# Up and down products of the later chunks: seven-product block sums in float32 exchanged for three float32r products

## The chip, the cores and the metric

The kernel runs on one core of a Trainium2 chip. The metric is the device time of one launch in microseconds, the median of several runs; smaller is better. The kernel before takes 517.86 us (two runs, 517.85 and 517.86). Its profiled execution has a span of 515.2 us from the first to the last instruction, and a mean granted TensorE clock of 0.992.

## The reference, cut to what matters

A gated linear-attention cell (mLSTM) for 4 batches and 8 heads of 40 channels over 768 steps is followed by a feed-forward layer with an exact GELU on 3072 tokens of 320 channels (8 x 40) and 2048 hidden channels.

```python
# q, k, v, o_gate: (4, 8, 768, 40); i_gate, f_gate: (4, 8, 768), float32
for t in range(S):
    m_new = np.maximum(f_gate[:, :, t] + m, i_gate[:, :, t])
    f_stab, i_stab = np.exp(f_gate[:, :, t] + m - m_new), np.exp(i_gate[:, :, t] - m_new)
    C = f_stab * C + i_stab * einsum('bhd,bhe->bhde', vt, kt)
    n = f_stab * n + i_stab * kt
    h_tilde = einsum('bhde,bhe->bhd', C, qt)
    y[:, :, t] = sigmoid(o_gate[:, :, t]) * h_tilde / max(|n . q|, 1)
# bridge: y as (3072, 320)
h = x @ w_in                                  # 320 -> 2048
g = 0.5 * h * (1.0 + erf(h / sqrt(2)))
out = g @ w_out                               # 2048 -> 320, float32
```

w_in and w_out arrive as 64-bit floats; the kernel reads their bits as 32-bit words and builds float32 numbers from them.

## The kernel before

The sequence is cut into six chunks (c = 0 to 5) of L = 128 steps for all four batches b, so one chunk is TG = 512 tokens of the feed-forward layer. For each chunk and batch a "cell" makes the attention output, in steps with one letter each: M mask, W weights (8 Exp on ScalarE), G gate (Sigmoid), T turn (8 transposes of k and q), S scores, C carry (state), V values, Y finish, X turn_y (3 transposes of y into xT). Strings of letters fix the order in which the steps are written, and each engine runs its own part of that order. The **front** is chunk 0's cells and products, the conversion of the weights (K, J) and chunk 1's cells. After it come five **stages**: stage c does the products of chunk c, with the cells of chunk c+1 between the down products.

Products of a stage, all in float32: the up product uses blocks of half the hidden channels by half the tokens and seven block products instead of eight, on sums of weight and x blocks; the last 64 of the 320 input rows are done apart, on half of the array's rows (w_rest). The down product likewise has seven half-width products.

```python
    HF, HT, HD = NF // 2, TG // 2, DM // 2          # 8, 256, 160
    def product(to, lhs, rhs, f0, first, last):     # up: 128 x 256 results
        for j in range(2):
            nc.tensor.matmul(to[:, j, :], lhs[:, (f0 + j) * P:(f0 + j + 1) * P], rhs, ...)
    def products(f0, to_sum):
        ...
        product(c11, a11, b11, f0, True, False)
        nc.scalar.copy(out=blk[1][1], in_=c11)
        product(c12, s2, t2, f0, True, True)
        nc.vector.tensor_tensor(out=blk[0][0], in0=c12, in1=blk[1][1], op=OP.add)
        ... (five more products, two more sums)
    def rest(f0, pair, h):                          # the last 64 input rows
        for j in range(2):
            for e in range(2):
                nc.tensor.matmul(pair[e][:, j, :], w_rest[halves[e], ...], xT[halves[e], NX, ...], ...)
    # down_steps: seven products; a step is one product for one of two token tiles t
            for j in range(HF):
                nc.tensor.matmul(bank[at][:, i, :], lhs(j, t), rhs(j), ...)     # 128 x 160
DOWN = """
    M0 Z M1 T0 W0 F F T1 W1 Z G3 Z F S0 Z S1 C0 M2 Z C1 G1 G0 M3 V0 Y0 Z V1 W2 Z F F T2 W3 F T3 F G2 Z Y1 S2 S3 C2
    V2 C3 Y2 V3 F F Y3 X0 F F X1 X2 F F X3 F"""
    for c in range(1, NCH):                         # one stage
        summed_up(g, ...)                           # all up products first
        steps = dict(F=in_turn(down_steps(c, g)), ...)      # 14 down steps
        if c + 1 < NCH:
            steps |= cell_steps(c + 1, "MWGTSCVYX")
        play(DOWN if c + 1 < NCH else "F " * 14, steps)
```

PSUM has eight banks in four pairs: ps_tr (tag "tr"), ps_h ("h"), and ps_mm with tags "a" and "b". In a cell, T and X take "tr" banks, C takes "h", V takes "a", and S takes "a" or "tr".

Of the kernel before, what the change touches and what calls it, by code (L numbers as in the profile page):

```python
# [9 lines left out]
F32 = mybir.dt.float32  # L10
BF16 = mybir.dt.bfloat16
# [4 lines left out]
P = 128  # L16

I23 = 2.0 ** 23

# [7 lines left out]
    I5 J c1 B5 I2 K y1 I4 I2 s2 x0 O4 L4 t3 J x1 B4 s3 v2 I7 g3 L5 g2 c2 c3 y2 v3 x2 O5 L6 K J G0 A y3 x3 J H M0 M1  # L27
    K K J T0 W0 O6 M2 O7 A J W1 S0 C0 K J T1 L7 U U K Z K V0 T2 A M3 J J G1 S1 K W2 W3 K C1 Z A S2 Z V1 G2 J Y0 J K
    C2 Z T3 J K Y1 U U J S3 Z V2 C3 K J K K J J F K F F F Z J K J X0 K K J F F F Z J F K G3 Y2 F J K V3 J K F K X1 J
    J F F F F K Z X2 B8 J F Y3 X3 B9 F"""  # L30
DOWN = """
    M0 Z M1 T0 W0 F F T1 W1 Z G3 Z F S0 Z S1 C0 M2 Z C1 G1 G0 M3 V0 Y0 Z V1 W2 Z F F T2 W3 F T3 F G2 Z Y1 S2 S3 C2
    V2 C3 Y2 V3 F F Y3 X0 F F X1 X2 F F X3 F"""
# [3 lines left out]
def kernel(  # L37
# [32 lines left out]
    NM = 2  # L70
    NB = 4
    WP = 512
    assert S % L == 0 and 3 * BH <= P and DFF % (4 * WP) == 0 and DM == NX * P + R and DM <= WP and D <= DP and NLD == B == 4

    const = ctx.enter_context(tc.tile_pool(name="const", bufs=1))
    wts = ctx.enter_context(tc.tile_pool(name="wts", bufs=B))
    raw = ctx.enter_context(tc.tile_pool(name="raw", bufs=2))
    two = ctx.enter_context(tc.tile_pool(name="two", bufs=2))
    outp = ctx.enter_context(tc.tile_pool(name="outp", bufs=2))
    dram = ctx.enter_context(tc.tile_pool(name="dram", bufs=1, space=bass.MemoryType.DRAM))  # L80
# [7 lines left out]

    w_in = const.tile([P, NX, 2, DFF // 2], F32, name="w_in")
    w_rest = const.tile([P, DFF // 2], F32, name="w_rest")
    w_out = const.tile([P, NF, DM], F32, name="w_out")
# [3 lines left out]
    xT = const.tile([P, NX + 1, TG], F32, name="xT")  # L98
# [31 lines left out]
    def load_M(n):  # L130

        if n >= NCH * B:
            return
        c, b = divmod(n, B)
        Mb[n] = wts.tile([P, H, L], F32, name="Mb", tag="Mb", bufs=NM)
        nc.sync.dma_start(out=Mb[n].rearrange("p h l -> p (h l)"),
                      in_=M_d[c - 1, b * H:(b + 1) * H, :].rearrange("h l -> (h l)").unsqueeze(0).to_broadcast([P, H * L]))
# [113 lines left out]
    for f in range(0, DFF // 2, WP // 2):  # L251
        for x in range(NX):
            pieces.append(([w_src["in"][x * P:(x + 1) * P, w_cols(e, f, WP // 2)] for e in range(2)],
                           w_in[:, x, :, f:f + WP // 2]))
        if f % WP == 0:
            pieces.append(([w_src["in"][NX * P:DM, w_cols(e, f, WP)] for e in range(2)], w_rest[:, f:f + WP]))
    n_in = len(pieces)
    for f in range(NF):
        pieces.append(([w_src["out"][f * P:(f + 1) * P, :]], w_out[:, f, :]))
# [32 lines left out]
    def conv_two(i):  # L292

        if i < len(pieces):
# [5 lines left out]
            if len(dst.shape) == 3:  # L300
                s, p = [t.rearrange("p (e f) -> p e f", e=2) for t in (s, p)]
# [20 lines left out]
    class Cell:  # L322
# [14 lines left out]
        def weights(self, b):  # L337

            n = self.c * B + b
            W[n] = wts.tile([P, H, L], F32, name="W", tag="W")  # L340
            if self.c > 0:
                M_n = Mb.pop(n)
# [17 lines left out]
            if self.c > 0 and not 2 * B <= n + NM < 2 * B + NM:  # L360
                load_M(n + NM)

# [17 lines left out]
        def weigh_values(self, b):  # L380
            vw = self.vw[b] = two.tile([P, H, D1], F32, name="vw", tag="vw")
# [3 lines left out]
        def scores(self, b):  # L385
# [3 lines left out]
            pool, tag = (ps_tr, "tr") if self.c > 0 and b % 2 else (ps_mm, "a")  # L389
# [10 lines left out]
        def carry(self, b):  # L400
# [4 lines left out]
            pf = ps_h.tile([P, H + NP, D1], F32, name="pf", tag="h")  # L405
# [10 lines left out]
            if c > 0:  # L416
# [4 lines left out]
                self.far[b] = two.tile([P, H, D1], F32, name="far", tag="far")  # L421
# [13 lines left out]
        def values(self, b):  # L435
# [3 lines left out]
            pool, tag = (ps_mm, "a") if self.c > 1 else (ps_h, "h")  # L439
# [39 lines left out]

# [313 lines left out]
```

## Time and profile before

| what | before |
|---|---|
| time | 517.86 us |
| span of the profiled execution | 515.2 us |
| TensorE (PE) busy | 500.3 us, 97% |
| VectorE (DVE) busy | 340.2 us, 66% |
| ScalarE (ACT) busy | 255.0 us, 49% |
| GpSimd (POOL) busy | 60.9 us, 12% |
| DMA | 41.62 MB, mean 81 GB/s |

The page gives, after the busy times, a map of the span in 40 slices, the DMA queues, the chain of work that ended last with its shares by engine and line, and the costliest groups of instructions. A line such as L682 is a line of the kernel's file. PE is the matmul stream, PEld the loading of the stationary operand. A float32 matmul of the program leaves two records in the trace: the 64 instructions `po<-w_out,g` of 320 columns in the front appear as 128 records. A record's own duration holds the time in which it overlaps its neighbours; the pace of a stream is read from the starts of successive groups in the timeline.

### The profile page before, as it was taken

Reading aid. Unit: us, or ns where it says so; the run is one execution under the profiler, and the core shown is the slowest. Engines: PE = TensorE matmul, PEld = TensorE weight load, DVE = VectorE, ACT = ScalarE, POOL = GpSimd, SP = SyncE. Lnnn points to the kernel's source line nnn. Section 1 sums busy time; section 2 is a strip of 40 time slices with the busy share of each in tenths; the row PEclk is TensorE's granted clock in tenths of the full one; section 3 lists DMA queues with packets and bytes.
Section 4 is the critical chain, followed back from the end, with each engine's and each line's share of the span. In section 5 each row is a group of like instructions: output and inputs, shape, how many; then the busy total and the mean of one; then the engine's idle time right before and its main releaser. Section 6 shows DMA issues by size and latency. Waiting matters only on the chain.

```text
span 515.2 us, 10957 instructions
## 1 busy us (share of the span) xinstructions
PE 500.3 (97%) x4472; PEld 450.6 (87%) x4472; DVE 340.2 (66%) x696; ACT 255.0 (49%) x523; POOL 60.9 (12%) x98
## 2 busy tenths in 40 slices
PE   4889999999999999999999999999999999999997
PEld 3778888767888999988999988999988999988997
DVE  7789598999577887347668347678347657237621
ACT  7696999555344960152980132982123882124300
POOL 3002100000210225000145000053000021000000
PEclk9799999999999999999999999999999999999999
DMA  6999751279900254900234900124920020000001
GB/s 128 223 214 212 184 147 53 64 163 171 198 0 1 84 116 58 167 0 2 74 88 69 167 28 1 43 83 81 166 52 2 5 80 1 27 27 0 1 2 51
DMA packets 111442, 41.62 MB, mean 81 GB/s; under 512 B 101184, under 2 KB 104416, under 8 KB 111392
## 3 DMA queue, kind: packets, MB, share of 16 engines
q1 hardware_dynamic: 111392, 40.92, 37.5%
q8 instruction: 35, 0.57, 0.5%
q14 instruction: 15, 0.12, 0.1%
HBM read 36.90 MB, written 4.01 MB: 79 GB/s over the span
## 4 chain that ended last, share of the span: by engine, by line
PE 91%; ACT 4%; DVE 3%; issue 0%; DMA 0%; SPq 0%; DVEq 0%; ACTq 0%
PE po L682 30%; PE pu L597 24%; PE pu L626 7%; PE po L659 7%; PE pu L538 5%; PE ps L395 4%; PE ph L444 4%; PE pt L373 4%; PE pf L419 2%; PE pf L414 2%; PE pu L544 1%; PE px L470 1%; ACT W L359 1%; ACT pow L285 1%; ACT pow L286 1%; DVE M L194 1%
## 5 line engine op out<-in xcount | busy, mean ns | idle before, releaser
L682 PE MATMUL po<-w_out,g 128*128 128x160 f32 x640 | 91.5, 299 | 0.0
L682 PEld LDWEIGHTS po<-w_out,g 128*128 128x128 f32 x640 | 88.0, 190 | 0.3 <-DVE g L639 0.3
L597 PE MATMUL pu<-xT,w_in 128*128 128x256 f32 x240 | 58.8, 381 | 0.0
L639 DVE TENSOR_TENSOR g<-pu,g 128x512 f32<-128x512 f32 x60 | 40.5, 689 | 22.4 <-PE pu L626 21.0
L597 PEld LDWEIGHTS pu<-xT,w_in 128*128 128x128 f32 x240 | 45.0, 190 | 7.5 <-ACT g L640 1.7
L471 ACT COPY xT<-px 128x384 f32<-128x384 f32 x24 | 11.1, 480 | 77.9 <-PE px L470 77.8
L359 ACT ACTIVATE W<-Mb,aT 128x128 f32<-128x128 f32 x160 | 48.9, 391 | 0.1
L682 PE MATMUL po<-w_sums,sums 128*128 128x160 f32 x320 | 47.3, 302 | 0.0
L398 DVE TENSOR_TENSOR W<-ps,W 128x512 f32<-128x512 f32 x48 | 30.2, 683 | 23.9 <-PE ps L395 21.2
L334 POOL TENSOR_SCALAR_AFFINE_SELECT Mb<-Mb 128x1024 f32<-128x1024 f32 x20 | 22.9, 1155 | 185.3 <-DMA Mb<-M_d 131.2
L682 PEld LDWEIGHTS po<-w_sums,sums 128*128 128x128 f32 x320 | 44.0, 190 | 0.4
L606 ACT COPY g<-pu 128x512 f32<-128x512 f32 x20 | 11.6, 582 | 58.2 <-PE pu L597 58.2
L695 DVE TENSOR_TENSOR o_sb<-po,o_sb 128x320 f32<-128x320 f32 (+1 forms) x27 | 12.5, 463 | 39.4 <-PE po L682 36.2
L637 ACT ACTIVATE g<-pu 128x512 f32<-128x512 f32 x20 | 12.0, 598 | 52.7 <-PE pu L626 52.7
L597 PE MATMUL pu<-x_sums,in_sums 128*128 128x256 f32 x160 | 37.8, 379 | 0.0
L626 PE MATMUL pu<-xT,w_rest 64*128 64x256 f32 x320 | 37.2, 382 | 0.0
L640 ACT ACTIVATE g<-g 128x512 f32<-128x512 f32 x60 | 36.1, 627 | 1.9
L608 DVE TENSOR_TENSOR g<-pu,g 128x512 f32<-128x512 f32 x20 | 13.8, 692 | 34.6 <-PE pu L597 28.8
L626 PEld LDWEIGHTS pu<-xT,w_rest 64*128 64x128 f32 x320 | 30.1, 187 | 6.4 <-issue 3.3
L659 PE MATMUL po<-w_out,g 128*128 128x320 f32 x128 | 35.7, 434 | 0.0
L597 PEld LDWEIGHTS pu<-x_sums,in_sums 128*128 128x128 f32 x160 | 30.2, 190 | 4.3
L659 PEld LDWEIGHTS po<-w_out,g 128*128 128x128 f32 x128 | 23.8, 190 | 9.3
(140 smaller groups left out, 884.3 us busy)
## 6 DMA issues: line engine op xcount, KB each, us to landing
Mb<-M_d SPq DMA_DIRECT2D x20, 512.0 KB, 3.7
bits<-in_moe_w_in_dram SPq DMA_DIRECT2D x20, 256.0 KB, 4.6
bits<-in_moe_w_out_dram SPq DMA_DIRECT2D x16, 320.0 KB, 3.0
vb<-in_v_dram SPq DMA_DIRECT2D x24, 160.0 KB, 4.9
ob<-in_o_gate_dram SPq DMA_DIRECT2D x24, 160.0 KB, 4.2
qb<-in_q_dram SPq DMA_DIRECT2D x24, 160.0 KB, 4.0
kb<-in_k_dram SPq DMA_DIRECT2D x24, 160.0 KB, 4.5
out_dram<-o_sb SPq DMA_DIRECT2D x24, 160.0 KB, 3.0
```

The lines of the kernel that those rows point to most:

```text
L334: nc.gpsimd.affine_select(out=t, in_=t, compare_op=OP.is_ge, fill=1.0e30, base=0, pattern=[[0, H], [1, L]], channel_multiplier=-1)
L359: nc.scalar.activation(out=W[n][:, h, :], in_=src, func=AF.Exp, scale=-1.0, bias=aT[:, self.c, r:r + 1])
L373: nc.tensor.transpose(pt[:, p, :], src[n % NLD][:, 2 * p:2 * p + 2, :].rearrange("p h d -> p (h d)"), ident)
L395: nc.tensor.matmul(ps[hip][:, p, :], kT[r, p, :], qT[r, p, :], start=True, stop=True)
L398: nc.vector.tensor_tensor(out=w, in0=ps[hip], in1=w, op=OP.mult)
L538: nc.tensor.matmul(banks[-1][e][:, i - i0, :], w_in[:, x, e, i * P:(i + 1) * P], xT[:, x, t0:t1], start=(x == 0 and i == i0), stop=False, ...
L597: nc.tensor.matmul(to[:, j, :], lhs[:, (f0 + j) * P:(f0 + j + 1) * P], rhs, start=(first and j == 0), stop=(last and j == 1), skip_group_c ...
L626: nc.tensor.matmul(pair[e][:, j, :], w_rest[halves[e], (f0 + j) * P:(f0 + j + 1) * P], xT[halves[e], NX, HT * h:HT * (h + 1)], start=False ...
L639: nc.vector.tensor_tensor(out=blk[e][h], in0=x, in1=y, op=OP.add),
L640: nc.scalar.activation(out=blk[e][h], in_=blk[e][h], func=AF.Gelu))
L659: nc.tensor.matmul(po[b], g.t[:, f, b * L:(b + 1) * L], w_out[:, f, :], start=(f == 0), stop=(f == NF - 1))
L682: nc.tensor.matmul(bank[at][:, i, :], lhs(j, t), rhs(j), start=(first and i == 0 and j == 0), stop=(i == n - 1 and j == HF - 1), skip_grou ...
```

## The change

The products of chunks 1 to 5 are no longer done by block sums. Each operand is split into float32r parts, `hi` (the number times 1 - 2^-13, written as float32r) and a remainder, and a product becomes three float32r products: hi with hi, lo with lo, and the "all" operands (hi + lo of the weights, x - hi of the activations), with scale factors chosen so that one accumulation gives the product and the evacuation multiplies by 4097. The front (chunk 0) keeps its float32 products, without block sums.

- **Up.** One tile is 128 hidden channels for all 512 tokens: six matmuls for the first 256 input rows (two row blocks by three parts). The last 64 rows of two of the parts are stacked to full 128-row operands, so that they take two matmuls more: eight matmuls of 512 columns.
- **Down.** One hidden tile, four batches, three parts: twelve matmuls of 320 columns, into four banks that stay open for the whole stage.
- **Order.** A stage has 16 up and 16 down tiles, played in four quarters: four up, then four down with the steps of the cells between them. Cells of the chunk after next begin in the fourth quarter (lower-case letters).
- **New element work.** Each hidden tile is split after its GELU (one ScalarE copy, two VectorE operations), the "all" weights are made again in every stage (make_in, make_out), x is split at turn_y, and the weights are split once, in the front's end and in stage 1.
- **Banks and buffers.** From c = 2 on scores take the "h" banks, which the up tiles use too, and carry and values take "tr". W and Mb share three buffers instead of four and two.

```diff
+QUARTERS = """
+    U U U U F V0 S1 C1 F G0 G1 G2 G3 Y0 W2 F T2 M3 F
+    U U U U F V1 S2 C2 F Y1 W3 F T3 m0 F
+    U U U U F V2 S3 C3 F Y2 w0 F t0 m1 F
+    U U U U F V3 s0 c0 F Y3 X0 X1 F w1 X2 X3 F t1 m2"""
+SECOND = """
+    M0 U M1 T0 U Z W0 U U F S0 C0 M2 T1 F W1 Z G0 G1 G2 G3 F V0 S1 C1 Z F Y0 W2 T2 M3
+    U U U U F V1 S2 C2 F Y1 W3 Z F T3 m0 F Z
+    U U U U F V2 S3 C3 F Y2 w0 Z F t0 m1 F
+    U U U U F V3 s0 c0 F Y3 X0 X1 F w1 X2 X3 F t1 m2"""
 ... (the front's string: the sums Z are gone, two splits of weights Z and the four X stand near its end)
-            pool, tag = (ps_tr, "tr") if self.c > 0 and b % 2 else (ps_mm, "a")
+            pool, tag = (ps_h, "h") if self.c > 1 else (ps_tr, "tr") if self.c > 0 and b % 2 else (ps_mm, "a")
 ... (carry and values: ps_tr "tr" if self.c > 1)
+    HI, LO = PART * 2.0 ** -12, -BASE * 2.0 ** 12
+    def split_weight(w, hi, lo):
+        nc.scalar.activation(out=hi, in_=w, func=AF.Copy, scale=HI)
+        nc.vector.scalar_tensor_tensor(out=lo, in0=hi, scalar=LO, in1=w, op0=OP.mult, op1=OP.add)
+    def both(out, hi, lo):
+        nc.vector.tensor_tensor(out=out, in0=hi, in1=lo, op=OP.add)
+    def split(x, hi, all_, lo):
+        nc.scalar.activation(out=hi, in_=x, func=AF.Copy, scale=PART)
+        nc.vector.tensor_tensor(out=all_, in0=x, in1=hi, op=OP.subtract)
+        nc.vector.scalar_tensor_tensor(out=lo, in0=x, scalar=-1.0 / BASE, in1=hi, op0=OP.mult, op1=OP.add)
+    def split_x(px, t):
+        hi, main = parts["x_hi"][:, :, t], slice(0, NX)
+        nc.scalar.activation(out=hi, in_=px, func=AF.Copy, scale=PART)
+        nc.vector.tensor_tensor(out=parts["x_all"][:, main, t], in0=px[:, main], in1=hi[:, main], op=OP.subtract)
+        for e, r in enumerate(halves):
+            nc.vector.tensor_tensor(out=parts["x_all"][r, NX + e, t], in0=px[r, NX], in1=hi[r, NX], op=OP.subtract)
+        for out, x, h in ((parts["x_lo"][:, :, t], px[:, main], hi[:, main]), (hi[r, NX], px[r, NX], hi[r, NX])):
+            nc.vector.scalar_tensor_tensor(out=out, in0=x, scalar=-1.0 / BASE, in1=h, op0=OP.mult, op1=OP.add)
+    class Stream:
+        def make_in(self, i):
+            both(self.in_all[i % 2], parts["in"][i], in_lo[i])
+        def make_out(self):
+            ...
+                if k < NF:
+                    split_out(f)
+                both(self.out_all[k % 3], parts["out"][:, f, :], out_lo[f])
+        def up(self):
+            pu = ps_h.tile([P, TG], F32, name="pu", tag="h")
+            ...
+            for n, (w, x) in enumerate(todo):                     # eight, 512 columns each
+                nc.tensor.matmul(pu, w, x, start=(n == 0), stop=(n + 1 == len(todo)), skip_group_check=True)
+            nc.scalar.activation(out=self.g[e], in_=pu, func=AF.Gelu, scale=4097.0)
+            split(self.g[e], *self.parts[k % 4])
+            if e == 0 and k + 2 < len(self.tiles):
+                self.make_in((i + 1) % HF)
+            ...
+        def down(self):
+            ...
+            for n, b in order:                                    # three parts by four batches, 320 columns
+                nc.tensor.matmul(self.po[b], self.parts[k % 4][n][:, b * L:(b + 1) * L], w_parts[n], ...)
+                if last and n == 2:
+                    ...
+                    nc.scalar.activation(out=o_sb, in_=self.po[b], func=AF.Copy, scale=4097.0)
+                    send(c, b, o_sb)
+            if self.made < self.done + 2:
+                self.make_out()
 ... (removed: in_sum, sum_x, summed_up, weight_sum, hidden_sums, down_steps and their buffers)
```

## Prediction

> **What bounds the kernel now.** I read the page's head and its chain first, then a table of busy time by stage (cut where the up products of each chunk begin), then the timeline of one stage.
>
> ```profile
> PE 500.3 (97%) x4472; PEld 450.6 (87%) x4472; DVE 340.2 (66%) x696; ACT 255.0 (49%) x523; POOL 60.9 (12%) x98
> PE 91%; ACT 4%; DVE 3%; issue 0%; DMA 0%; SPq 0%; DVEq 0%; ACTq 0%
> ...
> core 0: us, PE busy (x) PEld busy (x) DVE busy (x) ACT busy (x) POOL busy (x), PEclk, DMA share, GB/s
> ...
> 95.96:133.19 37.23, 37.23 (x173) 26.57 (x174) 32.77 (x89) 18.34 (x34) 0.00 (x0) 1.00 0.77 146
> 133.19:212.77 79.58, 79.58 (x765) 74.13 (x765) 57.27 (x119) 36.13 (x76) 18.70 (x24) 1.00 0.39 80
> 212.77:292.35 79.58, 79.58 (x765) 74.13 (x765) 49.46 (x88) 35.70 (x75) 14.44 (x20) 1.00 0.35 69
> 292.35:371.93 79.58, 79.58 (x765) 74.12 (x765) 49.05 (x88) 35.70 (x75) 12.78 (x18) 1.00 0.35 69
> 371.93:451.50 79.57, 79.57 (x710) 73.88 (x710) 43.91 (x82) 36.28 (x76) 5.39 (x6) 1.00 0.12 32
> 451.50:515.20 63.70, 60.45 (x392) 55.67 (x390) 28.79 (x42) 13.19 (x22) 0.00 (x0) 0.99 0.04 14
> ```
>
> The matmul stream is the bound, and from 57.6 us on it is so without a gap: in four stages PE is busy for the whole of the stage, and its clock is full. The other engines have slack, but the front's end less than the rest: DVE 32.8 of 37.2 us. A shorter matmul stream shortens the kernel until DVE, or a chain of waits, stops it.
>
> Busy PE is not peak PE, so the pace comes from starts in the timeline:
>
> ```profile
> 26.00 0.38 PE L356 MATMUL pm<-beyond,eye 128*128 128x512 bf16 x1
> 26.22 0.39 PE L354 MATMUL pm<-M_parts,row 96*128 96x128 bf16 x4
> ...
> 212.61 1.03 PE L597 MATMUL pu<-xT,w_in 128*128 128x256 f32 x4
> 213.47 1.89 PE L597 MATMUL pu<-x_sums,in_sums 128*128 128x256 f32 x8
> ...
> 240.72 3.72 PE L626 MATMUL pu<-xT,w_rest 64*128 64x256 f32 x32
> 244.38 0.65 PE L373 MATMUL pt<-ident,kb 128*128 128x128 f32 x4
> ...
> 250.53 2.34 PE L682 MATMUL po<-w_sums,sums 128*128 128x160 f32 x16
> 252.80 2.06 PE L395 MATMUL ps<-qT,kT 64*128 64x128 f32 x32
> ```
>
> Four float32 records of 256 columns take 213.47 - 212.61 = 0.86 us, 216 ns each; with two records per matmul a float32 matmul costs 432 ns, 1.69 ns a column. A bfloat16 matmul of 512 columns takes 26.22 - 26.00 = 0.22 us, 0.43 ns a column: a quarter.
>
> **What the Trainium skill says.** "FP8 and Floating Point Precision", TensorE Precision Notes: true FP32 is four passes through the array, while "FP32 reduced precision" reads the four bytes and truncates to FP22. The trace agrees with the four passes (1.69 against 0.43 ns). That float32r costs one pass is my reading of that note; no float32r matmul is in this trace. "TensorE: Matmul & The Clock Gate", Back-to-back issue gap: N/2.4 + 2.5 ns. That is 216 ns for 512 columns and 136 ns for 320; the two-pass records of 256 and 160 columns agree (216 ns, and 32 of them in 4.35 us of the chain, 136 ns, each with its own weight load). "VectorE: DVE Perf Modes", The perf-mode tier table: a float32 tensor_tensor runs at the 1x rate; here 512 elements take 681 to 692 ns. "ScalarE: Activation LUTs", Table sets: gelu, exp and sigmoid are anchors of different sets, and each switch needs a load; the trace has loads of 1283 ns.
>
> **The change, part by part.**
>
> *Matmuls removed.* Per stage: 56 up products at 432 ns = 24.2 us; the 64-row rests, two groups of 3.65 us = 7.3; 112 down products at two records of 136 ns = 30.4. Sum 61.9. The stage's 79.6 us leaves about 17.4 for the cells.
>
> *Matmuls added.* Up, 16 tiles x 8 x 216 ns = 27.6 us (a tile is 1.73). Down, 16 x 12 x 136 ns = 26.1 (a tile is 1.63). Sum 53.7, so 8.2 us less per stage and 41 us less over five, if nothing else waits.
>
> *ScalarE.* A tile costs a GELU (600 ns, from the row of g from pu) and a copy of 512 (about 590): 16 x 1.19 = 19.0. The cells take 32 Exp at 391 ns = 12.5, copies and gates 8.5, output copies 1.7; table loads rise to nine a stage (GELU and Exp in each quarter, Sigmoid once), 11.5. About 53 us of some 75: off the bound.
>
> *VectorE.* A tile costs 683 (x - hi) + 692 (lo) + half of 683 (make_in) + 485 (make_out, by the 320-wide product at L454) = 2.20 us, so 35.2 per stage. A batch's cell costs 2 x 683 (W) + 491 (far) + 495 (hs) + 2 x 321 (state) + 1766 (finish: 323 + 377 + 203 + 582 + 281) + x split. The split reads PSUM five times: 256 wide twice (about 425 ns, as at L587) and 64x128 three times (about 280, as M_left): 1.7. Sum 6.5, four batches 25.8. Steady stage: 61 us against 49 before, under PE's 71.
>
> *Stage 1* has more: 16 splits of w_out x 493 = 7.9, six of w_in x 692 and three stacked rests = 6.2, and five instead of four S and C (2.5). DVE: 77.7 us, PE: 53.7 + 21.2 (six T, five S and C) = 74.9. Here DVE is the bound.
>
> *The seam between stages.* The next up tile needs all of x, and X runs in the fourth quarter through two "tr" banks that V3 and c0 have just used and t1 needs next. I walk it by the durations above, from the end of the fourth up tile. PE: F 1.6, V3 2.5, s0 3.5, c0 4.6, F 6.2, X0 6.5, X1 6.9, F 8.5. DVE finishes the last hidden split at about 2.9, then make_out, hs, W, far, state and Y3 until 8.4; it splits X0 until 10.1 and X1 until 11.9. X2 can start only when X0's bank is free, 10.1, and X3 at 11.9; ScalarE meanwhile has w1 (load 1.28 + 8 x 0.39) until 12.0, so X2's and X3's hi come at 12.5 and 13.0, their splits end at 14.3 and 16.0, t1's second bank comes then, and the next U at 16.4. PE's own work there is 4 x 1.63 + 0.91 + 1.0 + 1.05 + 1.32 + 0.87 = 11.7. About 4.7 us lost at a seam, in four of them; in the last, without s0, c0, w1 and t1, about 4. The other quarters come out without a wait in the same walk: DVE needs 9.6 us after the last up tile, PE 10.4.
>
> *The front.* PE's work is the same. DVE in its last 37 us loses three or four sums of 0.68 and the four small ones of x, and gains four x splits (6.9), two w_in splits and one stacked rest (3.5): 32.8 grows to about 39, over 37. I allow 3 us: 136.
>
> *Sum.*
>
> | part | before | after |
> |---|---|---|
> | front | 133.2 | 136 |
> | stage 1 | 79.6 | 77.7 DVE + 5 of start and seam = 83 |
> | stages 2, 3 | 159.2 | 2 x (71.1 + 4.7 + 0.7) = 153 |
> | stage 4 | 79.6 | 53.7 + 12.3 + 4 = 70 |
> | stage 5 | 63.7 | 53.7 + 0.4 copy + 3 send = 57 |
> | sum | 515.2 | 499 |
>
> Stage 4 keeps two T, three S and C, four V and X. Stage 5's tail is a copy of 0.42 us and the 2.9 us that the end before took from the last sum (512.3) to 515.2. With the 2.7 us between span and time: 502 us.
>
> **The rivals.**
>
> 1. *The arithmetic is the gain.* Seams and DVE are hidden better than I walked them: 136 + 75 + 142 + 66 + 57 + 3 = 479. For it: PE is fully busy now, with DVE at 66%. Against: the bank chain of the seam, which is in the program's order of steps.
> 2. *VectorE becomes the bound.* If the operations with float32r output take longer than their float32 kin, or each step of the splits adds a wait, then every stage with cells goes to DVE's sum. With 15% on 61 us, a steady stage is 70 busy, plus 3 idle at the start of each quarter's up tiles while the first GELU runs: about 82. With 94 in stage 1 and 72 in stage 4 the total is near 525. For it: DVE works in step with PE in the up tiles (1.72 us against 1.73). Against: nothing in the operations differs but the output's type.
> 3. *float32r takes two passes or its weight load does not hide.* With two passes stages grow by 53.7 us each, to about 770; with a load that shows as 190 ns per down matmul (the length of a load record) by 10 us each, to 550. For it: no float32r matmul was traced; the transposes, also of four bytes, run at 109 ns per 128 columns, which could be two passes or the load. Against: the 160-column records at 136 ns already have a load each, so a load hides within 136 ns. I give this 5%.
>
> **Range and chances.** The gain of 41 us in matmuls is well founded if float32r is one pass. What is given back, 25 us by my sum, comes from walks with unmeasured steps, and can be 10 or 35. That gives 488 to 515, with 502 as the middle. Faster by over 2% means under 507.5: 0.70. Within 2%: 0.25. Slower: 0.05, nearly all rival 3.
>
> **What the profile after would show.** Pace: up tiles start 1.73 us apart in stage 5, down tiles 1.63, and stage 5 lasts near 57. Seam: PE idle before X2, X3, t1 or the first up tile of stages 2 to 5, released by DVE on x, some 4 to 5 us each; if there is none, rival 1. Stage 1 longest of all, with DVE over 90% busy; if DVE is over 90% in stages 2 and 3 as well, rival 2. A float32r matmul of 512 columns well over 220 ns from start to start would be rival 3. PE busy share lower than 97%. The prediction is wrong most likely in the size of the seam, or because quarters that I took as free wait for the "tr" banks too.

## The result, and the profile after

The changed kernel takes **564.06 us** (two runs, 563.96 and 564.16) against 517.86: a ratio of 1.089, 95% interval 1.0859 to 1.0922. It is slower, and 62 us over the prediction. The span is 561.9 us.

From the page of the kernel after: the line of busy times, the map of the granted clock in 40 slices, and the chain by engine.

```profile
PE 507.9 (90%) x4072; PEld 434.1 (77%) x4072; DVE 396.4 (71%) x844; ACT 333.1 (59%) x636; POOL 63.9 (11%) x100
PEclk9799989999888899989999979999999999999999
PE 40%; issue 23%; DVE 17%; ACT 11%; POOL 5%; DMA 4%; SPq 0%; POOLq 0%; DVEq 0%; ACTq 0%
```

The table of busy time by stage, cut where each chunk's up tiles begin; the first row is the end of the front.

```profile
core 0: us, PE busy (x) PEld busy (x) DVE busy (x) ACT busy (x) POOL busy (x), PEclk, DMA share, GB/s
95.96:146.42 50.46, 45.36 (x270) 32.43 (x269) 45.58 (x119) 24.16 (x43) 2.03 (x2) 0.93 0.49 119
146.42:248.66 102.24, 89.25 (x751) 77.92 (x749) 76.29 (x152) 70.38 (x139) 18.18 (x24) 0.93 0.29 57
248.66:336.21 87.55, 81.09 (x688) 71.31 (x685) 61.49 (x121) 50.74 (x95) 14.93 (x20) 0.96 0.32 63
336.21:419.76 83.55, 78.15 (x671) 68.40 (x670) 58.46 (x118) 50.40 (x95) 12.30 (x16) 1.00 0.32 66
419.76:496.29 76.53, 72.88 (x575) 63.80 (x574) 49.10 (x105) 39.37 (x70) 4.53 (x5) 1.00 0.03 12
496.29:561.90 65.61, 59.33 (x322) 51.70 (x320) 32.58 (x59) 22.32 (x38) 0.00 (x0) 1.00 0.06 21
```

There are 400 matmul records fewer than before, and yet PE is busy for 7.6 us longer. Before, PE was busy in the whole of each of the first four stages and made up 91% of the chain; now PE's idle time is 4 to 13 us in each stage, and PE is 40% of the chain. VectorE is at no more than 75% of any stage (76.29 of 102.24), so it isn't the bound of a stage by its sum. In the front's end it is nearly full, 45.58 of 50.46; experiment 15 asks whether that is what sets the front.

Two places show where it comes from. First stage 5, which has no cells. Columns of the timeline: start, length, engine, line, operation, number; in brackets the idle time before it and what ended that.

```profile
516.28 0.63 PE L667 MATMUL pu<-x_hi,w_in_hi 128*128 128x512 f32 x2
516.74 0.63 PE L667 MATMUL pu<-x_lo,w_in 128*128 128x512 f32 x2
517.87 0.74 PE L667 MATMUL pu<-x_all,in_all 128*128 128x512 f32 x2 [0.50 <-DVE in_all L514]
...
520.76 0.74 PE L688 MATMUL po<-parts_g 128*128 128x320 f32 x4
521.34 0.75 PE L688 MATMUL po<-w_rest,parts_g 128*128 128x320 f32 x4
```

Two matmuls of 512 columns take 0.46 to 0.47 us from start to start (0.43 by the pace that I used), and four of 320 take 0.58 (0.54): the stream is slower than I reckoned. And the all part of the quarter's third tile waits for `in_all`, the sum of two weight parts. From the start of x_lo to the start of x_all 1.13 us pass instead of 0.46; the bracket counts 0.50 of the 0.67 lost as idle.

Second the seam between two stages, here at the end of stage 1. The stage's last down tile finishes bank by bank, three parts each, so its matmuls are listed singly.

```profile
242.60 0.52 PE L483 MATMUL px<-ident,ob 128*128 128x128 f32 x3 [3.04 <-DVE x_hi L556]
244.34 0.88 PE L483 MATMUL px<-ident,ob 128*128 128x128 f32 x3 [1.22 <-DVE x_hi L556]
244.87 0.62 PE L688 MATMUL po<-parts_g,parts_more 128*128 128x320 f32 x1
245.28 0.47 PE L688 MATMUL po<-out_all,parts_more 128*128 128x320 f32 x1
245.55 0.47 PE L688 MATMUL po<-w_out,parts_more 128*128 128x320 f32 x1
...
247.54 0.31 PE L688 MATMUL po<-out_all,parts_more 128*128 128x320 f32 x1
247.69 0.31 PE L688 MATMUL po<-w_out,parts_more 128*128 128x320 f32 x1
```

X2 and X3 wait for VectorE to split X0 and X1 and so to free a bank: 4.3 us. After the wait the products run 270 ns apart, and only near 247.5 do they return to 150: the clock had been halved (granted clock 0.51 from 244.8 to 247.4 us), which costs more than a microsecond on top. The list of PE's waits by releaser (total us, times, longest) sums the two kinds over the kernel:

```profile
PE px L483 <- DVE x_hi L556: 13.5, 9, 3.3
PE pu L667 <- DVE in_all L514: 11.0, 19, 1.4
```

These totals hold idle time alone, not what a refill or a halved clock costs after it.

### The profile page after: what moved, and what is told of

Read it like the earlier page. It is cut to its first block, busy times and chain, and to the rows that moved or that the text cites. A ratio compares the mean times of both kernels' runs of the same rounds, so it can differ in the third digit from the quotient of the medians.

```text
span 561.9 us, 10476 instructions
## 1 busy us (share of the span) xinstructions
PE 507.9 (90%) x4072; PEld 434.1 (77%) x4072; DVE 396.4 (71%) x844; ACT 333.1 (59%) x636; POOL 63.9 (11%) x100
## 4 chain that ended last, share of the span: by engine, by line
PE 40%; issue 23%; DVE 17%; ACT 11%; POOL 5%; DMA 4%; SPq 0%; POOLq 0%; DVEq 0%; ACTq 0%
PE po L688 14%; PE pu L667 9%; PE pu L567 4%; PE ps L405 3%; PE ph L455 2%; ACT W L371 2%; PE pt L383 2%; ACT g L668 2%; DVE parts_g L543 2%; POOL W L348 2%; DMA vb<-in_v_dram 2%; DVE in_all L514 2%; DVE parts_g L544 1%; ACT parts_g L542 1%; DVE pow L313 1%
## 5 line engine op out<-in xcount | busy, mean ns | idle before, releaser
L668 ACT ACTIVATE g<-pu 128x512 f32<-128x512 f32 x80 | 47.9, 599 | 98.3 <-PE pu L667 98.2
L667 PE MATMUL pu<-x_all,in_all 128*128 128x512 f32 x160 | 52.7, 411 | 11.0 <-DVE in_all L514 11.0
L667 PE MATMUL pu<-x_hi,w_in_hi 128*128 128x512 f32 x160 | 51.8, 406 | 0.0
L667 PE MATMUL pu<-x_lo,w_in 128*128 128x512 f32 x160 | 51.0, 401 | 0.8 <-DVE x_lo L556 0.8
L371 ACT ACTIVATE W<-W,aT 128x128 f32<-128x128 f32 x160 | 48.9, 388 | 0.2
L613 PE MATMUL po<-w_out,first_g 128*128 128x320 f32 x128 | 38.2, 458 | 0.0
L386 ACT COPY kT<-pt 128x512 f32<-128x512 f32 x24 | 14.1, 586 | 35.8 <-PE pt L383 35.8
L688 PE MATMUL po<-parts_g,parts_more 128*128 128x320 f32 x160 | 35.2, 326 | 0.0
L688 PE MATMUL po<-w_out,parts_more 128*128 128x320 f32 x160 | 33.4, 315 | 0.0
L567 PE MATMUL pu<-first_x,w_in 128*128 128x256 f32 x128 | 30.8, 397 | 2.5 <-DVE w_in L316 1.6
L301 ACT ACTIVATE pow<-pow,e_hi 128x320 f32<-128x320 uint32 (+1 forms) x26 | 16.2, 621 | 26.9 <-DVE pow L299 26.9
L667 PE MATMUL pu<-x_all,rest_all 128*128 128x512 f32 x80 | 31.6, 395 | 0.0
```

What stands on the lines that cost most here:

```text
L301: nc.scalar.activation(out=p, in_=pu, func=AF.Relu, scale=-I23, bias=e_hi)
L371: nc.scalar.activation(out=W[n][:, h, :], in_=src, func=AF.Exp, scale=-1.0, bias=aT[:, self.c, r:r + 1])
L386: nc.scalar.copy(out=store[b], in_=pt)
L567: nc.tensor.matmul(banks[-1][e][:, i - i0, :], w_in[i][:, x, e, :], first_x[:, x, t0:t1], start=(x == 0 and i == i0), stop=False, skip_gro ...
L613: nc.tensor.matmul(po[b], first_g[:, f, b * L:(b + 1) * L], w_out[f], start=(k == 0), stop=(k == NF - 1))
L667: nc.tensor.matmul(pu, w, x, start=(n == 0), stop=(n + 1 == len(todo)), skip_group_check=True)
```

## The experiments

In the diffs, a plus is the experiment's line. "Quarter" is the time from one group of four up tiles to the next.

**1. The pace alone.** A kernel of nothing but matmul streams, four stationary tiles in turn.

```diff
+    stream("r512", wr, xr, 512, 48)     # float32r; then 320, 256 columns
+    stream("b512", wb, xb, 512, 48)     # bfloat16; then 320
+    stream("same512", wr, xr, 512, 48, True)   # one stationary tile throughout
```

> The pace of the matmul stream by itself: 48 matmuls each, stationary operand changed every time, nothing else running, real data. The output is not the reference's: only matmul streams run. If the slow pace seen in the changed kernel (232 ns per 512 columns, 146.6 per 320) belongs to float32r itself, the streams r512 and r320 show about 232 and 147 here too, while bfloat16 b512 and b320 show 216 and 136. If it comes from ScalarE and VectorE using SBUF beside it, r512 and r320 show 216 and 136 alone, and busy512, where both engines work, shows 232. If it is the weight load, same512 (one stationary operand) is faster than r512.

Timeline: the three float32r streams of 48 in one row, two of bfloat16, one of true float32 (256 columns), and float32r with one stationary tile; the row `mark` shows where that one ends, and the last row is float32r beside a busy ScalarE and VectorE.

```profile
21.32 24.05 PE L45 MATMUL r<-xr,wr 128*128 128x512 f32 x144
45.21 17.05 PE L45 MATMUL b<-xb,wb 128*128 128x512 bf16 x95
62.10 10.52 PE L45 MATMUL f<-x,w 128*128 128x256 f32 x48
72.27 11.27 PE L45 MATMUL same<-xr,wr 128*128 128x512 f32 x48
83.37 1.07 PE L45 MATMUL mark<-xr,wr 128*128 128x512 f32 x4
84.28 14.67 PE L45 MATMUL busy<-xr,wr 128*128 128x512 f32 x64
```

From start to start, bfloat16 takes (62.10 - 45.21) / 48 = 352 ns for 512 and 320 columns together, which is 216 + 136. float32r takes 23.89 / 48 = 498 ns for 512, 320 and 256 together; the single starts give steps of 227, 147 and 120 ns, and one step of 418 lifts the mean of the first to 231. With one stationary tile the step is 227 ns too (11.10 / 48 = 231 holds one of 420), and beside a busy ScalarE and VectorE (14.67 - 0.39) / 63 = 227. So **float32r is one pass** (256 columns in 120 ns, against 2 x 216 in true float32), **with about 11 ns more for each matmul**: the columns cost the same as in bfloat16 (227 - 147 = 80 ns for 192 columns, and 216 - 136 = 80), and 11 ns are added at 512 and at 320 columns alike. The other engines don't make the difference. The weight load is not excluded: the stream with one stationary tile still loads it before every matmul (48 load records of 188 ns; bfloat16's take 103). In the kernel after, a matmul of 512 columns takes 231.7 ns from start to start; the last 5 ns are not in the bare stream, and no run explains them.

**2. in_all ahead of the split.** VectorE's order changed, nothing else:

```diff
+            if e == 0 and k + 2 < len(self.tiles):
+                self.make_in((i + 1) % HF)
             split(self.g[e], *self.parts[k % 4])
-            if e == 0 and k + 2 < len(self.tiles):
-                self.make_in((i + 1) % HF)
```

> make_in written ahead of the hidden split, so that VectorE makes the next tile's sums before it waits for the GELU. Theory order: the wait of 0.5 us or more before the fourth pair of matmuls of the third up tile goes in all 20 quarters, 0.7 to 1.4 us each, so 13 to 20 us less, about 545 us. Rival, VectorE as a bound: the wait only moves to the down tiles or the seam, and the time stays within 4 us of 564.

548.15 us, ratio 1.059 (1.0572 to 1.0608): **15.9 us less**. In the third tile of stage 5's second quarter x_all now follows x_lo at the pace of the stream:

```profile
503.17 0.62 PE L667 MATMUL pu<-x_lo,w_in 128*128 128x512 f32 x2
503.63 0.63 PE L667 MATMUL pu<-x_all,in_all 128*128 128x512 f32 x2
```

The waits for in_all are gone, and a quarter without a seam takes 18.87 us instead of 19.64. That is PE's pure work: 4 x 8 x 232 ns + 4 x 12 x 147 ns = 14.5 us, which is the quarter measured in stage 5, plus the cells. The 19 waits cost some 0.8 us each.

**3. x copied out of its bank.** ScalarE copies the transposed y to SBUF, so that the bank comes free before VectorE's split.

```diff
+        xs = two.tile([P, NP, L], F32, name="xs", tag="kT")[:, 0:NX + 1, :]
+        nc.scalar.copy(out=xs, in_=px)
+        px = xs
```

> At turn_y, ScalarE first copies the three transposes out of PSUM, and the split reads the copy; the bank is free after one copy instead of after five VectorE operations. Theory banks: the waits of PE ahead of X2, X3 and in the front's end (13.5 us in all, released by x_hi) go, and with them most of the slow clock after them (0.93 in the front's end and stage 1, 0.96 in stage 2); 15 to 22 us less, about 545. Rival, VectorE's queue at the seam is the limit whoever holds the bank: the wait moves to the first up tile, and the gain is under 5 us.

563.14 us, ratio 1.0876 (1.0844 to 1.0909): no gain worth the name, where 15 to 22 us had been expected. PE's waits show why:

```profile
PE pu L670 <- DVE x_lo L559: 6.7, 5, 1.7
PE pt L383 <- ACT xs L552: 4.5, 6, 1.7
PE px L483 <- DVE ob L472: 4.3, 3, 3.3
```

The bank was one of two reasons. Without it, the first up tile of the next stage waits for the split itself (x_lo), and the transposes for the new copy (xs) and for Y3 (ob). A wait was exchanged for another.

**4. Both, and two small ones:** the third and fourth output copies in other buffers than o_sb's two, and stage 1's first W (its Exp needs a table load) after the fourth up tile instead of between the second and third.

```diff
-    M0 U M1 T0 U Z W0 U U F S0 ...
+    M0 U M1 T0 U Z U U W0 F S0 ...
```

> The two edits before, with the third and fourth output tile of a stage in buffers of their own (ScalarE waits 6.5 us in all for output transfers at the seams) and stage 1's W0 after its fourth up tile instead of between the second and third (PE waited 2.3 and 1.0 us for GELUs behind it). Theory order and banks: the gains add, 35 to 45 us, 520 to 530. Rival VectorE: stages 1 to 3 go to VectorE's own sums and the total stays over 540.

540.35 us, ratio 1.0441 (1.0417 to 1.0465): 23.7 us less than the kernel after, where 35 to 45 had been expected. Stage 1 went from 100.8 us in e2_in_first to 89.8, and 7.7 of these 11 us lie in its first quarter, where W0 was moved (35.8 to 28.1 us; 36.0 in e3_x_copy); in the kernel after, W0's table load and Exp had stood ahead of the next GELU, so that PE waited 3.3 us for g. Stage 2 gained 2.4 us, and stages 3 to 5 lost 1.2 to 2.6: as in e3_x_copy, the copy of x moved a wait into the next stage's first quarter (stage 3's went from 19.1 to 22.2 us).

**5. The order in the fourth quarter.** V3 and Y3 moved together, the four X after them.

```diff
-    U U U U F V3 s0 c0 F Y3 X0 X1 F w1 X2 X3 F t1 m2
+    U U U U w1 F V3 Y3 s0 c0 F X0 X1 X2 F X3 F t1 m2
```

> The combined edit of before, with the fourth quarter played in another order: w1's eight Exp right after the up tiles, Y3 right after V3, and the four X before the last down tile with nothing of ScalarE between them. Theory chain: at the seam the fourth quarter (22.6 us against 18.9 of a steady one) and the quarter after it (20.9 to 22.2) wait for a chain w1, x_hi, x split; with w1 out of it each of the four seams loses 2 to 4 us, 526 to 533 us. Rival, VectorE's seven us of x splits is the chain itself: under 1 us a seam, 537 to 540.

536.64 us, ratio 1.0383 (1.0352 to 1.0414): 3.7 us less, under the 7 to 14 expected and next to the 537 to 540 of the rival. PE still waits 7.2 us for x_lo, five times.

**6. and 7. Relief for VectorE through GpSimd, and for the front.** e6_x_on_gpsimd is e5_order with the differences x - hi on GpSimd; e7_front also moves one weight split from the front to the start of stage 1.

```diff
-        nc.vector.tensor_tensor(out=parts["x_all"][:, main, t], ...)   # and the two on 64 rows
+        nc.gpsimd.tensor_tensor(out=parts["x_all"][:, main, t], ...)
```

> e5 with the three x - hi differences of a split moved from VectorE to GpSimd, which is idle at the seam. Theory VectorE-bound seam: each batch takes 1.0 us off VectorE, 4 us a seam and 4 in the front's end, of which about half shows: 8 to 12 us under e5, near 518. Rival, the two engines hinder each other in SBUF (VectorE operations of 0.17 us took 0.5 to 1.05 us beside GpSimd in the changed kernel's trace): no gain or a loss.

> e6 with the second weight split taken out of the front's end and put at the start of stage 1, where VectorE waits for the first GELU. Theory front: 0.7 us of VectorE less in the front, where it is the bound, 1 us or less in the total; 516 to 518. A larger gain would say that the front's end has a chain that I don't see.

542.25 us (1.0475; 1.0459 to 1.049) and 545.27 (1.0537; 1.0521 to 1.0553): both **slower** than e5_order. On VectorE the difference took 421 ns (256 columns) and 302 (64 rows). On GpSimd (groups by shape: count, busy us, mean ns), and x_lo on VectorE beside it:

```profile
L557 POOL TENSOR_TENSOR x_all<-xs,x_hi 64x128 fp32r<-64x128 f32 x40 | 21.5, 539 | 1.5
L555 POOL TENSOR_TENSOR x_all<-xs,x_hi 128x256 fp32r<-128x256 f32 x20 | 17.5, 873 | 71.0 <-ACT x_hi L554 68.1 <-PE px L483 1.9
...
L559 DVE SCALAR_TENSOR_TENSOR x_lo<-xs,x_hi 128x256 fp32r<-128x256 f32 x20 | 12.6, 628 | 1.1 <-ACT x_hi L554 0.7
```

That makes 0.87 + 2 x 0.54 = 1.95 us in a row instead of 1.02, on the path that the seam waits for. And the rival of the expectation, that the two engines hinder each other, shows as well: x_lo took VectorE 628 ns (418 to 862) instead of 425 in e5_order. The two are not separated. e7_front is 3.0 us slower than e6_x_on_gpsimd: stage 1 began no earlier (143.9 against 142.9), and its first quarter was 2.5 us longer, so the weight split found no room there.

**8. The parts in bfloat16.** e4_combined with `F32R = bfloat16`. The parts are coarser, so this is another rounding of the same three products, with the same number of instructions.

> The combined edit with bfloat16 instead of float32r for all parts. This gives up precision (the parts no longer add up to the operand) and is no replacement; it has the same instructions in the same order with bfloat16 operands. Theory pace: up matmuls go from 232 to 216 ns and down matmuls from 147 to 136, so the steady quarter goes from 18.87 to 18.05 us (16 x 0.016 x 2 + 48 x 0.0106 less), stage 5's quarter from 14.45 to 13.4, and the total falls by 16 to 22 us to about 520. Rival, the pace is hidden behind other engines: the total falls by less than 8.

518.05 us, ratio 1.0015 (0.9993 to 1.0036): 22.3 us less than e4_combined. Stage 5's quarter goes from 14.46 to 13.42 us, the steady quarter from 18.87 to 17.75. The pace is shown in place: some 1.1 us in each of 20 quarters.

**9. and 10. V3 and Y3 a quarter earlier.** With them in the third quarter, all X can come at once in the fourth. To save VectorE work, the two differences on 64 rows became part of one, and the stacked tails of the weights were then multiplied on 64 rows only. e10_seam_front also moves a product of chunk 1's Y to GpSimd.

```diff
-    U U U U F V2 S3 C3 F Y2 w0 F t0 m1 F
-    U U U U w1 F V3 Y3 s0 c0 F X0 X1 X2 F X3 F t1 m2
+    U U U U F V2 S3 C3 F Y2 w0 F V3 Y3 F t0 m1
+    U U U U F X0 X1 w1 s0 c0 F X2 F X3 F t1 m2
-                     (parts["rest_all"][:, m], parts["x_all"][:, NX + e])]
+                     (parts["rest_all"][halves[e], m], parts["x_all"][halves[e], NX])]
```

> The combined edit, with V3 and Y3 moved up into the third quarter, so that the four X of the fourth can follow its up tiles at once (X0 X1 w1 s0 c0, X2, X3, one down tile between), and with the differences x - hi made in one operation of 384 columns: the last rows' product uses 64 of the array's rows and needs no zero-padded copy. VectorE then has about 12.4 us in the fourth quarter against 11.4 of PE (in e5 some 16). Theory VectorE-bound seam: the fourth quarter falls from 21 to about 19 us and the one after it from 20.7 to about 19, three seams and the last give 12 to 16 us, near 522. Rival, the bank pair of the transposes still binds: less than 5 us under e5.

> e9 with the first product of Y of chunk 1 on GpSimd instead of VectorE. Theory front: the front's end, where VectorE is busy 45 of 50 us, gets about 2 us shorter (4 x 0.48), near 520. Rival, as with the x differences on GpSimd: a slower producer in a chain costs more than it frees, 522 or more.

552.24 us (1.0675; 1.0656 to 1.0694) and 554.68 (1.0723; 1.0696 to 1.0749). PE's waits at the seams of all stages came to some 3 us in e9_seam, against some 12 in e5_order, and the kernel was still slower than e5_order by 16 us. The product on GpSimd in e10_seam_front gained nothing (stage 1 begins at 143.4 against 143.1). Timeline of stage 5 in e9_seam, where nothing but products runs:

```profile
503.12 0.40 PE L667 MATMUL pu<-x_hi,rest_turned 128*128 128x512 f32 x1
503.45 0.50 PE L667 MATMUL pu<-x_all,rest_all 64*128 64x512 f32 x1
503.88 0.73 PE L667 MATMUL pu<-x_hi,w_in_hi 128*128 128x512 f32 x2
504.44 0.62 PE L667 MATMUL pu<-x_lo,w_in 128*128 128x512 f32 x2
504.90 0.63 PE L667 MATMUL pu<-x_all,in_all 128*128 128x512 f32 x2
```

The matmul on 64 rows starts 0.33 us after the one ahead of it, and the next starts 0.43 after that, where 0.23 is the pace; the pair that follows takes 0.56 instead of 0.46. No wait is named. A tile takes 2.25 us instead of 1.85. So 64 rows between 128 cost 0.40 us each time, while PE counts as busy.

**11. The waits filled.** The kernel after, with 54 matmuls of 128 columns, whose result nobody reads, ahead of X2 and X3 in three seams, so that the clock isn't lowered.

```diff
+                    for _ in range(count):
+                        nc.tensor.matmul(spare[:, 0:P], ident, ident, start=True, stop=True, ...)
```

> The changed kernel with 54 unread matmuls of 128 columns into a spare bank ahead of X2 and X3 of chunks 1 to 3, sized to the waits of PE there (about 0.2 us each). They do no work; they keep TensorE busy while it waits. Theory clock: the stretches at half clock after these waits (clock 0.79 in the front's last 16 us, 0.88 and 0.77 at the first two seams) go, some 6 to 9 us less than 564. Rival, the clock is not driven by these waits: no gain, or up to 3 us more from the added matmuls.

561.18 us, ratio 1.0851 (1.083 to 1.0872). The clock of the profiled execution rose from 0.966 to 0.981, and 2.9 us were gained of 6 to 9 expected; the interval still touches that of the kernel after (1.0859 to 1.0922). Around the two seams the clock is back at 1.00 (0.93 and 0.86 before the filling), but the fourth quarters that end there are only 0.0 and 1.3 us shorter and the quarters after them 0.8 and 0.1. The halved clock is a small term of its own; most goes with the waits.

**12. x split once.** e5_order, with VectorE's split of x left out for chunks 2 to 5; their products use the low parts of chunk 1.

> e5 with the VectorE part of the x split left out for chunks 2 to 5 (x_all and x_lo keep chunk 1's values; only hi is made anew), so its output is not the reference's. Theory: what is left at the seams is VectorE's split of x, and without it the three steady seams and the last go to PE's own sum, 4 us each, near 520. That would say that the change with its seams gone only draws level with the kernel before. Rival, the seam is set by something else (banks, the table loads of ScalarE): less than 6 us.

522.54 us, ratio 1.0102 (1.0086 to 1.0119): 14.1 us less. This is what VectorE's split of x on the path was still worth at the seams of e5_order; with that left out, the kernel is still 1.0% slower than the kernel before.

**13. and 14. Full rows again.** e9_seam's order with e5_order's split of x, and with 128 rows in every product of an up tile; e14_seam_bf16 is the same in bfloat16.

```diff
-                     (parts["rest_all"][halves[e], m], parts["x_all"][halves[e], NX])]
+                     (parts["rest_all"][:, m], parts["x_all"][:, NX + e])]
```

> e9_seam with one thing undone: the last product of an up tile uses all 128 rows again (the stacked tails with the half-zero block of x_all), instead of 64 rows. Theory A (what made e9_seam slow is the 64-row matmul among 128-row ones): in e9_seam's stage 5 an up tile came every 2.25 us, in e5_order's every 1.85, 0.40 more on each of 80 tiles, 32 us, while its waits at the seams were almost gone. So about 520 us, steady quarters back at 18.9, and the quarter across each seam at 19 to 21. Theory B (the early V3 and Y3 crowd VectorE, and the 0.40 has to do with that): then over 535, with the steady quarters still above 20.

> e13_seam_full_rows with the parts in bfloat16 instead of float32r (coarser parts, another rounding of the same three products). From e4_combined to e8_bf16_parts this took 22 us. Theory A (pace of float32r is a term of its own, added to the waits): about 498 us, steady quarter 17.75, stage-5 quarter 13.4. Theory B (with the seams filled VectorE, at some 17 us of each 19 us quarter, becomes what bounds the steady quarters): about 510, steady quarters near 18.5.

**530.48 us**, ratio 1.0258 (1.0243 to 1.0274), the fastest with float32r and all of its work, and **509.45 us**, ratio 0.9848 (0.9831 to 0.9864), 1.5% under the kernel before, though with coarser parts. The rows were what made e9_seam slow: steady quarters are back at 18.87, stage 5's at 14.45. Only 21.8 us came back instead of 32, since the quarters that wait for VectorE gained less than 1.6 us each: the first of stage 1 gained 0.4, and the last ones of stages 1 and 2 became 1.9 and 0.2 us longer. That VectorE's split, longer again, does this is likely but not shown apart. e14_seam_bf16 has the quarters of the first theory (17.75 and 13.42) and the total of the second. The table by stage of e13_seam_full_rows:

```profile
143.37:235.10 91.73, 84.91 (x751) 74.05 (x749) 78.65 (x159) 70.37 (x143) 17.98 (x24) 0.98 0.32 63
235.10:315.94 80.84, 78.75 (x688) 70.83 (x686) 62.03 (x121) 52.65 (x98) 14.84 (x20) 0.98 0.35 69
315.94:392.84 76.90, 76.76 (x670) 68.83 (x669) 56.91 (x113) 51.45 (x97) 12.19 (x16) 1.00 0.33 66
392.84:466.12 73.28, 71.97 (x575) 64.11 (x574) 51.11 (x110) 42.12 (x76) 4.59 (x5) 1.00 0.05 17
466.12:528.90 62.78, 58.24 (x322) 52.01 (x320) 33.04 (x60) 22.13 (x38) 0.00 (x0) 0.99 0.06 21
```

Stage 3 has PE busy for 76.76 of 76.90 us: its seam is all but closed by order alone (0.8 us of waiting for x_lo is left in the first tile of stage 4). Stage 2's still shows a wait, and shows how the clock follows it:

```profile
311.42 0.52 PE L483 MATMUL px<-ident,ob 128*128 128x128 f32 x3 [2.09 <-DVE state L444]
...
312.26 0.31 PE L691 MATMUL po<-parts_g,parts_more 128*128 128x320 f32 x1
312.41 0.31 PE L691 MATMUL po<-out_all,parts_more 128*128 128x320 f32 x1
312.55 0.43 PE L691 MATMUL po<-w_out,parts_more 128*128 128x320 f32 x1
312.78 0.47 PE L691 MATMUL po<-parts_g,parts_more 128*128 128x320 f32 x1
313.05 0.47 PE L691 MATMUL po<-out_all,parts_more 128*128 128x320 f32 x1
```

After the wait PE comes to full pace (150 ns) and drops to 270 ns only 1.1 us after it had resumed; the granted clock is 1.00 from 311.4 to 312.5 us and 0.53 in the 1.8 us that follow. At the same place in e9_seam a wait nearly as long is followed by steps of 150 ns throughout, with no drop:

```profile
318.20 0.52 PE L483 MATMUL px<-ident,ob 128*128 128x128 f32 x3 [1.90 <-DVE state L444]
...
320.06 0.31 PE L688 MATMUL po<-out_all,parts_more 128*128 128x320 f32 x1
320.20 0.31 PE L688 MATMUL po<-w_out,parts_more 128*128 128x320 f32 x1
```

**15. The front.** e13_seam_full_rows with chunk 1's split of x taken from VectorE: ScalarE writes plain copies in place of VectorE's differences.

> e13_seam_full_rows in which, for chunk 1 alone, ScalarE fills x_all and x_lo with plain copies of x instead of VectorE's differences (so the low parts of chunk 1 are not what they should be; the number of matmuls is the same). It takes 4 x 1.7 us = 7 us off VectorE in the front's last 45 us and puts as much on ScalarE, which is busy for half of that time. Theory A (the front is bound by VectorE at its end: 21.5 of 24 us busy): stage 1 starts some 5 to 7 us earlier, at 137 to 138 instead of 143.4, and the time is about 525. Theory B (the front waits in a chain of steps, transposes, ScalarE and loads, and VectorE is only busy beside it): the start moves by less than 2 us, time 529 to 531.

531.64 us, ratio 1.026 (1.0237 to 1.0283). VectorE was busy for 18.6 of the 24 us from 119 to 143 us instead of 21.5; stage 1 began at 142.0 instead of 143.4, and its first quarter was 2.3 us longer. VectorE's sum by itself does not set the front's end; a wait of 2.3 us for Y's last product (ob) was left, and the clock in the last 24 us was 0.93. Since ScalarE's copies stand in the same row of steps as VectorE's differences did, this doesn't say what the split costs as a part of that row.

## Why the prediction was wrong, point by point

The way from the kernel after to the prediction, by the runs:

| step | time, us | gain |
|---|---|---|
| after | 564.1 | |
| in_all ahead of the split (e2) | 548.2 | 15.9 |
| bank, output buffers, place of W0 (e4) | 540.4 | 7.8 |
| order of V3, Y3 and X (e13) | 530.5 | 9.9 |
| pace of bfloat16 for the parts (e14) | 509.5 | 21.0 |
| predicted | 502.0 | 7.5 left |

The rows are what the edits gained, not the errors of the forecast: the sum had 18 us for the seams in it, which e13_seam_full_rows saves in part. The errors show part by part (us; the kernel before had 133.2, 79.6, 159.2, 79.6 and 63.7):

| part | predicted | after | e14_seam_bf16 |
|---|---|---|---|
| front | 136 | 146.4 | 144.2 |
| stage 1 | 83 | 102.2 | 87.7 |
| stages 2, 3 | 153 | 171.1 | 147.9 |
| stage 4 | 70 | 76.5 | 68.6 |
| stage 5 | 57 | 65.6 | 58.8 |

**The matmuls added** ("16 x 8 x 216 ns", "16 x 12 x 136 ns") were the term mis-sized most. Counts were right, the pace was not: 128 x 231.7 + 192 x 146.6 ns = 57.8 us a stage instead of 53.7, some 20 over five. The gain in matmuls is therefore about 20 us, not 41. The formula of the Trainium skill, "TensorE: Matmul & The Clock Gate", Back-to-back issue gap, gives bfloat16's 216 and 136 ns as e1_pace measured them; I carried it over to float32r, for which it does not hold here. The page gives the formula for an isolated matmul, and about 131 ns at 512 columns for a sustained stream; no stream here came near that, so the measured 216 stands. Rival 3 named the type as the risk but allowed only for two passes or a load that shows with its whole 190 ns. It was neither; whether the 11 ns belong to the load is open.

**"The other quarters come out without a wait"** was wrong: the kernel after has 19 waits for in_all, nearly one in each quarter. The walk added up VectorE's work after the last up tile and did not follow the first: its GELU, its copy to hi and two VectorE operations stood ahead of make_in, whose result the third tile needs. By the durations of the trace that is 1.85 (tile) + 0.60 (GELU) + 0.6 (hi) + 1.38 (split) + 0.69 (make_in) = 5.1 us, against 2 x 1.85 + 4 x 0.23 = 4.6 until the third tile's in_all part. e2_in_first shows the price, 15.9 us; none of it was in the sum. I had named these quarters as a likely place of error, but for another reason, the "tr" banks.

**The seam** held better than the rest. The bank chain of X2 and X3 is there, as walked, with 3.0 + 1.2 us of waiting at the end of stage 1 against 4.7. Stages 3 and 4 of the kernel after are 7.1 and 6.5 us over the sum; the pace takes 4.1 of each and in_all 3.2 (they last 80.3 and 73.4 us in e2_in_first), so their seams cost about what the walk said. By the same reckoning stage 2 has 3 us more, with the clock at 0.88 in its last quarter. What the walk lacked is the halved clock afterwards, and that the bank was not the only gate: e3_x_copy freed the bank and gained 1 us, and only the earlier V3 and Y3 closed stage 3's seam.

**Stage 1** was to be bound by VectorE's sum. That sum was right (76.3 us against 77.7), but the stage took 102.2 us instead of 83: it waited in chains. The walk missed W0's table load among the GELUs, worth 7.7 us in the first quarter (e4_combined), and about 6 us are left after this, the pace and in_all.

**The front** (136 predicted, 146.4 measured, 143.4 in e13_seam_full_rows) was mis-sized by 7 to 10 us, and this is still there in e14_seam_bf16, where stage 1 begins at 144.2. That the last row of the first table has nearly the same size is a coincidence: in that run stages 1 and 5 are 6.5 us over the forecast and the other stages 6.5 under it. PE's matmuls there are as many as before, as I wrote, but VectorE's work from 96 us on was 45.6 us instead of the 39 of the forecast. But in e13_seam_full_rows the first of chunk 0's 128 down records starts at 100.5 us against 95.9 before, and they end 5.7 us further behind; their waits are for the weights (w_out) and for Y (ob). Which step of the weights' conversion, the Y and the splits sets this is not settled: e15_front_x_on_act speaks against VectorE's sum alone, and I tried no other order of the front. One candidate was left untried: the change also cuts the buffers of `vw`, the weighted v that the carry step multiplies, from two to one. In the kernel after VectorE waits for that buffer for 6.9 us in the front (5.1 of them up to 76.2 us; no such wait is in the trace before), and from 60 to 80 us it is busy for 11.3 us instead of 16.2.

**Right:** VectorE takes no longer for 512 columns of float32r output than for float32 (681 to 692 ns before), against rival 2, and its sums in the steady stages (61.5 and 58.5 us against 61). The sums of 320 columns in make_out were slower than reckoned, 535 to 561 ns against 485. In the kernel after:

```profile
L543 DVE TENSOR_TENSOR parts_g<-g,parts_g 128x512 fp32r<-128x512 f32 x40 | 27.7, 691 | 76.4 <-ACT parts_g L542 76.4
L544 DVE SCALAR_TENSOR_TENSOR parts_g<-g,parts_g 128x512 fp32r<-128x512 f32 x40 | 27.3, 683 | 0.0
```

Stage 1 was the longest, as predicted; but DVE was busy for 75% of it, not 90.

As a whole the forecast took an estimate of the gain from one end (41 us) and of the loss from walks at a few places (25 us). The gain was 20, and the losses in the order as written some 66: the measured change is 46 slower. "Slower" had a chance of 0.05, nearly all of it for rival 3; the cause that weighed as much as the pace, a chain inside the quarters, stood in no rival.

## What to carry to other kernels

In the kernel before, all up products of a stage stood together, and no wait of PE showed in four stages. Cut into groups of four tiles that feed each other through ScalarE and VectorE, each group's first result became a deadline. Write down, for each group, the chain from its first tile to the first consumer, not only the sum of work: putting one 0.69 us operation ahead of two others was worth 16 us. Measure the pace of a number type in a bare stream before building a gain on it: 11 to 16 ns a matmul halved the gain here. And look at the pace of a stream before and after matmuls of fewer rows are put into it, since PE counts as busy either way.

## What the runs showed of the hardware that was not expected

- **float32r** streams 512, 320 and 256 columns in 227, 147 and 120 ns (e1_pace), bfloat16 512 and 320 in 216 and 136: the same 80 ns for 192 columns, and 11 ns more for each matmul. float32r's 227 holds with one stationary tile or four; in the kernel after it was 232.
- **A matmul on 64 rows among matmuls on 128** cost 0.40 us each time (tile of 2.25 against 1.85 us). The Trainium skill, "TensorE: Matmul & The Clock Gate", Step-by-step: what each phase is for, says that the next weights load during the running matmul when the row groups don't conflict or the load goes to the background buffer, and that the row count doesn't matter to the load's time. The added time could be a load that isn't hidden, but no run here separates the load from the matmul.
- **Half clock after short waits.** The same page, What's actually happening, gives half the clock after an idle window of about 3.4 us. Here 4.3 us of waiting broken by three transposes were followed by 270 ns a matmul, and in e13_seam_full_rows a single wait of 2.1 us was too, with the drop 1.1 us after the work had resumed. In e9_seam a wait of 1.9 us at the same place was followed by none, so these runs give no length from which on the clock drops.
- **GpSimd** took 873 ns for a difference of 256 columns for which VectorE took 421, and an operation of VectorE in the same step (x_lo) went from 425 to 628 ns.
